# Splitting a 640-point transform by residue mod 4 in an adaLN, spectral filter and FFN block, with hand-ordered engines

## The chip, the cores and the metric

The kernel runs on one core of one Trainium2 chip. The metric is device microseconds of one execution; smaller is better.

Engines as the profile names them: PE is TensorE (matmuls), PEld its weight loads, DVE is VectorE, ACT is ScalarE, POOL is GpSimd, SP is the engine that issues DMAs. PEclk is the granted TensorE clock as a share of full speed.

## The reference, cut to what matters

The block takes scales and shifts for two layer norms from a conditioning vector `c` (this is adaLN), filters the tokens in the frequency domain, and ends in a feed-forward network (FFN).

```python
# x: [1, 2048, 640] bf16
mod = (silu(c) @ w_mod).reshape(1, 6, 1, 640)
sa, ca, ga, sb, cb, gb = mod[:, 0] ... mod[:, 5]

h = layernorm(x) * (1 + ca) + sa
X = rfft2(h)                              # over 2048 rows and 640 columns
y = irfft2(X * (w_r + 1j * w_i))          # w: [2048, 321]
x = x + ga * y

h = layernorm(x) * (1 + cb) + sb
x = x + gb * ((silu(h @ w_gate) * (h @ w_up)) @ w_down)   # 640 -> 1728 -> 640
```

The 2048 rows are held as 128 partitions times 16 values of t. The transform over the rows is done as a 128-point stage over the partitions, a 16-point stage over t, and twiddle factors folded into the 128-point tables.

## The kernel before: the parts that matter here

There are four stages.

1. Forward. For each of 16 tiles t: LayerNorm 1, five PE transposes, the transform over the 640 columns (`dfwd`), the 128-point stage (`s1`).
2. Filter. For each group of four columns: the 16-point matrix (`KS2`), the complex product with the filter on VectorE, the inverse 16-point matrix.
3. Inverse. For each tile: the 128-point stage (`vps`), the inverse column transform (`ops`), and the residual add that makes `x1`. LayerNorm 2 of the first quarter of the tiles is interleaved.
4. FFN, in four quarters of four tiles.

```python
def dfwd(t, hT):                       # forward: 10 matmuls of 324 columns
    zps = ps1.tile([P, 2, 512], F32, name="zps")
    for h in range(2):
        for c5 in range(NC5):
            nc.tensor.matmul(zps[:, h, :L], lhsT=hT[:, c5, :], rhs=Rs[:, c5, h * L:(h + 1) * L],
                             start=(c5 == 0), stop=(c5 == NC5 - 1))
    # ... Z <- zps, on VectorE or ScalarE

def stage_a(q):                        # filter, four columns
    # ... xps <- B2 times KS2
    for cp in range(2):
        in0 = xps5[:, :ni, cp].unsqueeze(2).to_broadcast([P, ni, 2, NT, 4])
        s0 = 1 - cp
        in1 = Wb[:, s0:s0 + 2, :, 16 * q:16 * q + 4 * ni].rearrange("p a k (i j) -> p i a k j", j=4)
        nc.vector.tensor_tensor(PP[:, :ni, cp], in0, in1, ALU.mult)   # L417: four neighbouring l innermost

# inverse, tile t
for h in range(2):
    ops = ps3.tile([P, 320], F32, name="ops", bufs=3)
    for ci in range(5):
        nc.tensor.matmul(ops[:], lhsT=VT[:, ci, :], rhs=Rinv_sb[:, ci, h * 320:(h + 1) * 320], ...)
    nc.vector.tensor_tensor(x1[:, t, h * 320:(h + 1) * 320], ops[:],
                            x_sb[:, t, h * 320:(h + 1) * 320], ALU.add)

# LayerNorm 2's scale and shift, on the transposed tile: columns 0, 2, 4 on VectorE, 1, 3 on ScalarE
nc.vector.tensor_scalar(h2T[:, :, c5, :], h2T[:, :, c5, :], one_p_cb[:, c5:c5 + 1], modcols[:, 2, c5:c5 + 1], ...)

# the fold of gb into w_down: 14 tensor_tensor on VectorE (L575), inside the first FFN quarter
```

## Time and profile before

| | us |
|---|---|
| before, median of the first 3 runs | 321.55 (320.47 to 322.75) |
| profiled execution, span | 319.9 |
| forward, to the first filter matmul | 65.4 |
| filter | 37.2 |
| inverse | 35.1 |
| FFN | 182.2 |

The windows view of before gives the busy time of each engine in each stage. The columns are the stretch and its length in us, then busy us of each engine with its count of instructions, the granted clock, the DMA share and GB/s.

```profile
core 0: us, PE busy (x) PEld busy (x) DVE busy (x) ACT busy (x) POOL busy (x), PEclk, DMA share, GB/s
10.50:65.40 54.90, 49.18 (x410) 33.47 (x411) 34.47 (x113) 32.09 (x59) 8.54 (x16) 0.94 0.60 219
65.40:102.50 37.10, 25.78 (x340) 21.80 (x341) 28.21 (x64) 24.02 (x46) 4.65 (x6) 0.91 0.52 127
102.50:137.70 35.20, 31.68 (x321) 24.63 (x321) 31.65 (x109) 13.35 (x20) 0.54 (x2) 1.00 0.39 137
137.70:319.90 182.20, 177.70 (x988) 96.44 (x987) 74.44 (x169) 40.28 (x66) 1.57 (x3) 1.00 0.11 27
```

TensorE is busy for 90% of the forward and inverse stages and 98% of the FFN; in the filter stage it is not, and VectorE is the busiest engine there.

### The profile page before, as it was taken

The page shows a single profiled execution, that of the slowest core. Times are in us where ns is not written, and L with a number is a line of the kernel's source. Part 1 is how long each engine was busy: PE and PEld are TensorE (multiplying, and loading weights), DVE is VectorE, ACT ScalarE, POOL GpSimd, SP SyncE. Part 2 cuts the span into 40 slices and gives each one's busy share as a digit, 9 for nine tenths or more (in the row PEclk, how much of TensorE's full clock was granted, in tenths as well). Part 3 has the DMA queues.
Part 4 walks back from the last instruction along what each step waited for, and adds up shares of the span by engine and source line. Part 5 has one row for each costly group of instructions (what it writes and reads, how often), then busy time and mean ns, then how long its engine had stood idle before and what let it go on. Part 6 is the DMA issues. An engine that isn't in the chain of part 4 may idle for free.

```text
span 319.9 us, 5193 instructions
## 1 busy us (share of the span) xinstructions
PE 285.4 (89%) x2087; PEld 177.4 (55%) x2087; DVE 172.9 (54%) x469; ACT 114.5 (36%) x197; POOL 16.3 (5%) x33
## 2 busy tenths in 40 slices
PE   0699879858666998888999999999999999999995
PEld 0477556647555786643446744457544467444574
DVE  2889563268984799899934432333233322333321
ACT  4477722745777433424222032211222200322200
POOL 1503001000202000000000000000000000000000
PEclk9999987987999999999999999999999999999999
DMA  7995900785513903113004100022100001000011
GB/s 272 416 394 203 298 29 12 287 149 119 208 72 108 423 25 61 25 36 56 0 2 102 41 31 0 1 54 71 49 2 0 0 23 41 31 0 0 0 43 41
DMA packets 26600, 29.81 MB, mean 93 GB/s; under 512 B 19521, under 2 KB 22546, under 8 KB 26450
## 3 DMA queue, kind: packets, MB, share of 16 engines
q1 hardware_dynamic: 22882, 12.66, 14.3%
q0 software_dynamic: 3040, 16.02, 13.8%
q10 hardware_dynamic: 656, 0.82, 0.9%
q8 instruction: 16, 0.26, 0.3%
q14 instruction: 6, 0.05, 0.0%
HBM read 21.86 MB, written 2.62 MB: 77 GB/s over the span
## 4 chain that ended last, share of the span: by engine, by line
PE 66%; DVE 16%; ACT 8%; DMA 7%; issue 1%; POOL 1%; SPq 0%; ACTq 0%; DVEq 0%
PE ups L567 17%; PE gps L564 16%; PE zps L314 4%; DMA Wb<-in_A_w_i_dram 4%; DVE x_1516 L536 3%; ACT Ep L436 2%; DMA x_sb<-in_A_x_dram 2%; DVE Wd_sb L575 2%; DMA h2T_all<-xn2c 2%; DVE xn2c L490 1%; PE yps L426 1%; PE yps L425 1%; PE gps L551 1%; PE xps L410 1%; PE gps__661 L362 1%
## 5 line engine op out<-in xcount | busy, mean ns | idle before, releaser
L571 DVE TENSOR_TENSOR AT<-ups,sg 128x512 bf16<-128x512 f32 x52 | 35.7, 689 | 63.2 <-PE ups L567 63.2
L567 PE MATMUL ups<-h2T_all,Wgu 128*128 128x512 bf16 x260 | 64.4, 379 | 1.3 <-DVE AT L571 1.3
L564 PE MATMUL gps<-h2T_all,Wgu 128*128 128x512 bf16 x260 | 64.4, 379 | 0.0
L570 ACT ACTIVATE sg<-gps 128x512 f32<-128x512 f32 x52 | 31.0, 597 | 73.1 <-PE gps L564 70.3
L587 PEld LDWEIGHTS <-AT 128*128 128x128 bf16 x448 | 43.8, 98 | 17.8
L567 PEld LDWEIGHTS <-Wgu 128*128 128x128 bf16 x260 | 25.4, 98 | 32.0 <-issue 1.5
L564 PEld LDWEIGHTS <-Wgu 128*128 128x128 bf16 x260 | 25.4, 98 | 30.7
L314 PE MATMUL zps<-Rs,hT 128*128 128x324 bf16 x160 | 29.4, 327 | 1.2 <-ACT hT L307 0.8
L417 DVE TENSOR_TENSOR PP<-xps,Wb 128x512 bf16<-128x512 f32 (+1 forms) x42 | 27.4, 662 | 5.4 <-ACT B_946 L405 1.8
L534 PE MATMUL ops<-Rinv_sb,VT 128*128 128x320 bf16 x160 | 24.4, 299 | 2.6 <-ACT VT L523 1.4
L314 PEld LDWEIGHTS <-hT 128*128 128x128 bf16 x160 | 16.1, 105 | 7.7 <-ACT hT L307 1.0
L534 PEld LDWEIGHTS <-VT 128*128 128x128 bf16 x160 | 15.0, 98 | 8.1 <-ACT VT L523 1.7
L523 ACT CAST VT<-vps 128x640 bf16<-128x640 f32 x16 | 10.8, 691 | 17.3 <-PE vps L521 17.3
L536 DVE TENSOR_TENSOR x_1516<-ops,x_sb 128x320 f32<-128x320 f32 x32 | 14.8, 471 | 2.2 <-PE ops L534 2.2
L307 ACT COPY hT<-t1ps 128x640 bf16<-128x640 bf16 x16 | 11.1, 697 | 6.4 <-PE t1ps L305 6.4
L329 ACT CAST A_sb<-aps 128x648 bf16<-128x648 f32 x16 | 11.2, 699 | 4.9 <-PE aps L328 4.7
L425 PE MATMUL yps<-identb,PP 128*128 128x128 bf16 x81 | 12.5, 233 | 0.0
L426 PE MATMUL yps<-identb,PP 128*128 128x128 bf16 x81 | 12.5, 233 | 0.0
L499 ACT ACTIVATE h2T_all<-h2T_all,modcols,one_p_cb 128x512 bf16<-128x512 bf16 x8 | 6.1, 806 | 14.2 <-DMA h2T_all<-xn2c 14.2
L318 DVE CAST Z<-zps 128x648 bf16<-128x648 f32 x8 | 6.5, 817 | 7.4 <-PE zps L314 5.8
L283 DVE BATCH_NORM_STATS2 st<-x_sb 128x6 f32<-128x320 bf16 x16 | 7.5, 470 | 5.5 <-DMA x_sb<-in_A_x_dram 5.5
L305 PE MATMUL t1ps<-identb,xn 128*128 128x128 bf16 x80 | 8.5, 237 | 2.2 <-POOL Ktab L229 2.2
(341 smaller groups left out, 387.1 us busy)
## 6 DMA issues: line engine op xcount, KB each, us to landing
wm<-in_w_mod_dram POOLq DMA_DIRECT2D x1, 3200.0 KB, 16.3
out_dram<-xo SPq DMA_DIRECT2D x16, 160.0 KB, 1.8
Wgu<-in_B_w_gate_dram POOLq DMA_DIRECT2D x1, 2160.0 KB, 9.1
Wgu<-in_B_w_up_dram POOLq DMA_DIRECT2D x1, 2160.0 KB, 14.9
Wd_sb<-in_B_w_down_dram POOLq DMA_DIRECT2D x1, 2080.0 KB, 9.9
x_sb<-in_A_x_dram SPq DMA_DIRECT2D x3, 640.0 KB, 8.4
Gtab<-tab_G SPq DMA_DIRECT2D x4, 384.0 KB, 8.8
Htab<-tab_H POOLq DMA_DIRECT2D x1, 1536.0 KB, 6.7
```

The source lines that it names most:

```text
L314: nc.tensor.matmul(zps[:, h, :L], lhsT=hT[:, c5, :], rhs=Rs[:, c5, h * L:(h + 1) * L], start=(c5 == 0), stop=(c5 == NC5 - 1))
L329: nc.scalar.copy(A_sb[:, :, t, :, :].rearrange("p l c j -> p c l j"), aps[:, :, :L].rearrange("p c (l j) -> p c l j", j=4),)
L417: nc.vector.tensor_tensor(PP[:, :ni, cp], in0, in1, ALU.mult)
L425: nc.tensor.matmul(yps[:, i, :], lhsT=PP[:, i, 0].rearrange("p a k j -> p (a k j)"), rhs=identb[:], start=True, stop=False)
L426: nc.tensor.matmul(yps[:, i, :], lhsT=PP[:, i, 1].rearrange("p a k j -> p (a k j)"), rhs=identb[:], start=False, stop=True)
L534: nc.tensor.matmul(ops[:], lhsT=VT[:, ci, :], rhs=Rinv_sb[:, ci, h * 320:(h + 1) * 320], start=(ci == 0), stop=(ci == 4))
L536: nc.vector.tensor_tensor(x1[:, t, h * 320:(h + 1) * 320], ops[:], x_sb[:, t, h * 320:(h + 1) * 320], ALU.add)
L564: nc.tensor.matmul(gps[:], lhsT=Wgu[:, 0, c5, fc * 128:(fc + 1) * 128], rhs=h2T[:, :, c5, :], start=(c5 == 0), stop=(c5 == NC5 - 1))
L567: nc.tensor.matmul(ups[:], lhsT=Wgu[:, 1, c5, fc * 128:(fc + 1) * 128], rhs=h2T[:, :, c5, :], start=(c5 == 0), stop=(c5 == NC5 - 1))
L570: nc.scalar.activation(sg[:], gps[:], ACT.Silu)
L571: mul_i = nc.vector.tensor_tensor(AT[:, fc, :], ups[:], sg[:], ALU.mult)
L587: nc.tensor.matmul(ops4[:], lhsT=AT[:, fc, tl * 128:(tl + 1) * 128], rhs=Wd_sb[:, fc, h * 320:(h + 1) * 320], start=(fc == 0), stop=(fc == ...
```

## The change

The intent is to take work off TensorE in the two stages that it bounds. The 640 columns are split by their residue mod 4, so that each residue has a short transform. The radix-4 butterfly that would put them together is folded into the 16-point matrices of the filter stage, where it costs no matmul. Forward, 1304 columns are streamed per tile instead of 3240; inverse, 1280 instead of 3200. A 16-point block now holds a column `l` and its partners `l+160` and, mirrored, `320-l` and `160-l`, so the products read the filter in pairs 160 elements apart and need a second, reversed copy (`Wv`), which is made by DMA through DRAM. Results of the inverse come out ordered by residue.

LayerNorm 1 is folded away too: its mean is corrected in `Z` and its `rstd` scales the table `G`, on GpSimd. Other work moves to GpSimd: LayerNorm 2's normalise of the first quarter, and the fold of `gb` into `w_down`, which before ran on VectorE during the FFN. All DMAs but one, the first load from `w_mod`, go to one queue. SBUF is laid out by hand in regions (`rX` x, `rM` products and x1, `rA` A_sb and w_down, `rE` tables and the inverse's input, `rW` filter and then FFN weights and h2T, `rL` small buffers).

```diff
 # forward
-        for h in range(2):
-            for c5 in range(NC5):
-                nc.tensor.matmul(zps[:, h, :L], lhsT=hT[:, c5, :], rhs=Rs[:, c5, h * L:(h + 1) * L],
-                                 start=(c5 == 0), stop=(c5 == NC5 - 1))
+        for h in range(2):
+            o_all = zps[0:M, h, 0:2 * RC]
+            nc.tensor.matmul(o_all, lhsT=lhs[4], rhs=R[:, 1, 2 * h:2 * h + 2, :].rearrange("p r n -> p (r n)"), ...)
+            for rr in range(2):
+                nc.tensor.matmul(zps[0:M, h, rr * RC:(rr + 1) * RC], lhsT=lhs[2 * h + rr], rhs=R[:, 0, 2 * h + rr, :], ...)
+        if t >= 2:
+            Gss[t - 2] = gscale(t - 2)                 # GpSimd, L323
+        ...                                            # Z, and the variance, on VectorE
+        nc.gpsimd.tensor_tensor(rstd[:, t:t + 1], vt, mhalf[:], ALU.pow)   # L341
 ... (cut)
 # filter products
-        in1 = Wb[:, s0:s0 + 2, :, 16 * q:16 * q + 4 * ni].rearrange("p a k (i j) -> p i a k j", j=4)
-        nc.vector.tensor_tensor(PP[:, :ni, cp], in0, in1, ALU.mult)
+        for hl in range(2):
+            in0 = xv[:, :n, hl, cp].unsqueeze(2).to_broadcast([P, n, 2, NT, 2])
+            if hl == 0:
+                in1 = _rev(Wn, base + ls[0], [[st, n], [NT * NW, 2], [NW, NT], [160, 2]])
+            else:
+                in1 = _rev(Wv, base + 255 - ls[0], [[-st, n], [NT * NW, 2], [NW, NT], [-160, 2]])
+            nc.vector.tensor_tensor(PP[:, :n, cp, hl], in0, in1, ALU.mult)   # L470
 ... (cut)
 # inverse
-            nc.vector.tensor_tensor(x1[:, t, h * 320:(h + 1) * 320], ops[:], x_sb[:, t, h * 320:(h + 1) * 320], ALU.add)
+            dv = "p (m h r) -> p h r m"
+            nc.vector.tensor_tensor(x1[:, t, :].rearrange(dv, h=2, r=2),
+                                    ops[:, :, 0:320].rearrange("p h (r m) -> p h r m", r=2),
+                                    x_sb[:, t, :].rearrange(dv, h=2, r=2), ALU.add)     # L649
 ... (cut)
+            if t == 9:
+                ln2_norm_pool()
+                for tl in range(4):
+                    ln2_xn(tl, nc.gpsimd)
+                ln2_tr(0)
+            if t == NT - 1:
+                ln2_mod(0)                             # L616, L619: scale and shift h2T
+        for f2 in range(NFC):                          # before: on VectorE, in the first FFN quarter
+            m = 128 if f2 < 13 else 64
+            nc.gpsimd.tensor_tensor(Wd_sb[:m, f2, :], Wd_sb[:m, f2, :], gb_bc[:m, :], ALU.mult)   # L663
```

## The prediction

> **What bounds it now.** The timeline of TensorE splits the 319.9 us into four stages.
> - Forward transform, to about 65 us. Per tile t: five transposes, ten 324-column matmuls (1.38 us start to start), four more (0.55): 2.2 us, TensorE back to back. Set-up takes 12 us; about 10 us is lost from 30 to 53 us, around the 11.9 us filter load in the chain of waits, the modulation matmuls and a clock of 0.76 to 0.81 (windows).
> - Filter, 66 to 102.5 us. VectorE paces it: 0.67+0.67+0.17 us per four columns, 1.51 us period, 21 times.
> - Inverse, 102.5 to 137.7 us. TensorE: ten 128-column matmuls 0.056 us apart and ten 320-column ones 0.136 us apart, 1.91 us per tile; plus stalls around LN2.
> - FFN, 137.7 us to the end: 44.36 us per quarter, matmuls back to back (last three quarters 133.1 us); the first quarter loses 1.6 us to the Wd fold on VectorE.
>
> The Trainium skill ("TensorE: Matmul & The Clock Gate", back-to-back issue gap) gives N/2.4+2.5 ns; the trace agrees (0.136 us at 320 columns, 0.056 at 128).
>
> **What changes.** The residue split makes the d transforms sparse: 1304 streamed columns per tile instead of 3240 forward, 1280 instead of 3200 inverse. That saves about 0.82 us of TensorE per tile each way, 13 us + 13 us. The radix-4 butterfly rides in the existing 16-point matrices: the filter stage keeps its 81 blocks, matmul count and products (0.67 us each). LN1's normalise pass, bn_stats and sqrt go; a sum of squares, five tiny operations and a scaling of G on GpSimd come.
>
> **By stage.**
> - Forward: TensorE falls to about 1.35 us per tile. ScalarE (hT 0.70 + A_sb 0.70 + half a Square 0.75) and VectorE (Z 0.82, half a square-sum 0.75, five tiny at 0.15) are both near 1.8. I take 1.9 to 2.0 with latencies, start near 11 us, plus 2 us for sa: ends near 47 us (saves 18).
> - Filter: VectorE needs 27 us of products, but the depth is one group: xps(g+1) queues behind two yps/copy/eps rounds, about 2.9 us per eight columns. The ga, gb, cb modulation matmuls move in (6 us). 36 to 38 us, nothing saved. Extra DMA: the filter is copied reversed through DRAM and read twice in 512-byte rows. From the old 642-byte load (4096 rows in about 11 us) I estimate 8 to 10 us for each of flip, normal and reversed read. All queue on SP ahead of wm_r (3.3 MB), tables and the transposes. wm_r lands near 54, transposes near 60: a stall of about 5 us. Ends near 91.
> - Inverse: 1.15 us per tile, but the LN2 sums on ScalarE make the first four 2.2 to 2.3. 24 us. LN2 of chunk 0 starts at tile 9 (GpSimd normalise 4 us, transpose 4.9 us): about 3 us stall. FFN starts near 118.
> - FFN: 4 x 44.36 + 3.2 = 180.7 us. Wd fold on GpSimd: the skill ("GPSIMD Engine Reference", elementwise accounting) has two-input operations at about 2.6 cycles per element; estimate 1.4 us x 14, hidden behind the 29 us before the first down projection.
>
> Sum: about 298 us.
>
> **Right or wrong in the profile.** Forward period under 2.1 us, TensorE gaps released by ScalarE and VectorE; filter stage near 37 us, DMA releasing gps/B2 reads; ops line near half its busy time; FFN quarters of 44.4 us.
>
> **What would make it wrong.** Slower: 512-byte DRAM-to-DRAM flips, a 4096-element GpSimd negation, TensorE dropping to its low clock in the thinner stages. Faster: DMA early enough, filter loop at VectorE's 2.66 us.
>
> Predicted 298 us, 8 in 10 between 285 and 310; faster by over 2%: 0.92, within 2%: 0.06, slower: 0.02.

## More of the kernel before

The groups view names the costly work: line, engine, operation, output and input, count; then busy us and mean ns of one; then idle time of the engine just before it and what ended that.

```profile
L314 PE MATMUL zps<-Rs,hT 128*128 128x324 bf16 x160 | 29.4, 327 | 1.2 <-ACT hT L307 0.8
L417 DVE TENSOR_TENSOR PP<-xps,Wb 128x512 bf16<-128x512 f32 (+1 forms) x42 | 27.4, 662 | 5.4 <-ACT B_946 L405 1.8
L534 PE MATMUL ops<-Rinv_sb,VT 128*128 128x320 bf16 x160 | 24.4, 299 | 2.6 <-ACT VT L523 1.4
L536 DVE TENSOR_TENSOR x_1516<-ops,x_sb 128x320 f32<-128x320 f32 x32 | 14.8, 471 | 2.2 <-PE ops L534 2.2
L496 DVE TENSOR_SCALAR h2T_all<-h2T_all,one_p_cb,modcols 128x512 bf16<-128x512 bf16 x12 | 4.3, 405 | 4.4 <-DMA h2T_all<-xn2c 4.4
```

L314 and L534 are the column transforms that the change makes sparse. Keep three other numbers in mind for later: a filter product (L417), a residual add (L536, 471 ns for 320 elements) and LayerNorm 2's scaling (L496, 405 ns for 512). The mean of L417 mixes two shapes; the view by form has the products of 512 elements alone at 681 ns:

```profile
L417 DVE TENSOR_TENSOR PP<-xps,Wb 128x512 bf16<-128x512 f32 x40 | 26.9, 681 | 5.3 <-ACT B_946 L405 1.8 <-PE xps L410 1.6 <-PE yps L426 0.6
```

## The result, and the profile after

| | median us | runs |
|---|---|---|
| before | 321.01 | 4, 318.42 to 322.75 |
| after | 337.36 | 4, 335.92 to 337.81 |

The ratio is 1.0535 with a 95% interval of 1.0463 to 1.0607: 5% slower. (A ratio here is the mean time of one kernel's fast runs over that of the other's of the same rounds, so it is not quite the ratio of the medians quoted.) The prediction of 298 us was wrong in sign, and 39 us too low.

The windows view of after, with stretches cut at the same events (the first cut lies 0.2 us before the first filter matmul, at 54.3); the fourth stretch is new:

```profile
10.50:54.10 43.60, 29.16 (x277) 21.22 (x276) 28.11 (x97) 24.79 (x43) 24.00 (x34) 0.99 1.00 324
54.10:104.30 50.20, 34.21 (x413) 27.33 (x413) 41.58 (x56) 34.59 (x49) 19.19 (x23) 0.84 0.50 106
104.30:135.50 31.20, 20.76 (x256) 17.99 (x256) 20.36 (x21) 16.96 (x32) 9.39 (x9) 0.94 0.42 133
135.50:149.90 14.40, 0.01 (x1) 0.04 (x2) 14.40 (x2) 1.52 (x2) 14.34 (x12) 0.50 0.00 0
149.90:334.10 184.20, 180.58 (x988) 97.28 (x988) 82.88 (x195) 39.93 (x66) 1.84 (x4) 0.98 0.11 27
```

The TensorE saving came: 49.2 busy us fell to 29.2 in the forward stage and 31.7 to 20.8 in the inverse. The stages did not follow. Forward fell by 11.1 us and the inverse by 3.9; the filter stage grew by 12.8 (37.2 to 50.0), 14.4 us of almost nothing came before the FFN, and the FFN grew by 2.0. Together that is 14.2 us, the difference of the two spans (334.1 against 319.9).

The groups of after that answer to those of before:

```profile
L470 DVE TENSOR_TENSOR rM<-xps,rW 128x512 bf16<-128x512 f32 (+2 forms) x44 | 38.4, 950 | 3.3 <-PE xps L458 3.3
L649 DVE TENSOR_TENSOR rM<-ops,rX 128x640 f32<-128x640 f32 x16 | 19.6, 1332 | 8.0 <-PE ops L646 8.0
L616 DVE TENSOR_SCALAR rW<-rW,one_p_cb,modcols 128x512 bf16<-128x512 bf16 x12 | 18.5, 1598 | 1.5 <-DMA rW<-rL 1.5
L663 POOL TENSOR_TENSOR rA<-rA,gb_bc 128x640 bf16<-128x640 bf16 (+1 forms) x14 | 18.9, 1393 | 0.0
L674 PE MATMUL gps<-rW,Wp_1292 128*128 128x512 bf16 x20 | 6.0, 440 | 17.4 <-DVE rW L616 17.4
L351 PE MATMUL aps<-rE 128*128 128x324 bf16 x16 | 5.0, 313 | 12.2 <-POOL rE L323 12.2
```

The mean of L470 again mixes shapes. By form, its products of 512 elements alone:

```profile
L470 DVE TENSOR_TENSOR rM<-xps,rW 128x512 bf16<-128x512 f32 x36 | 33.9, 1021 | 3.3 <-PE xps L458 3.3
```

Four things stand out. A filter product of 512 elements takes 1021 ns where it took 681. A residual add takes 1332 ns for 640 elements where two of 320 took 942. The mean scaling of h2T is 1598 ns where it was 405. And TensorE waits 17.4 us for that scaling, and 12.2 us for GpSimd's scaling of `G`.

The mean of L616 hides its shape. Of twelve instructions the shortest took 404 ns, the median 409 and the longest 14128. The timeline of after around that one (start, length, engine, line, idle time before with what ended it):

```profile
133.25 16.23 POOL L663 TENSOR_TENSOR rA<-rA,gb_bc 128x640 bf16<-128x640 bf16 x12
135.50 1.52 ACT L619 ACTIVATE rW<-rW,modcols,one_p_cb 128x512 bf16<-128x512 bf16 x2 [4.03 <-DMA rW<-rL]
135.50 15.35 DVE L616 TENSOR_SCALAR rW<-rW,one_p_cb,modcols 128x512 bf16<-128x512 bf16 x3 [1.47 <-DMA rW<-rL]
149.89 2.29 PE L674 MATMUL gps<-rW,Wp_1292 128*128 128x512 bf16 x5 [17.40 <-DVE rW L616]
```

ScalarE does two of the five scalings in 1.52 us. VectorE starts its first at the same moment and is done with it only when GpSimd's last fold is (133.25 + 16.23 = 149.48). The chain of waits of after in that stretch (start, length, what) has the same story:

```profile
127.99 2.58 POOL rL L605 x3
130.58 0.03 POOL rA L663
130.60 4.88 DMA rW<-rL
135.48 0.03 issue
135.50 14.14 DVE rW L616
149.64 0.25 issue
149.89 2.29 PE gps L674 x5
```

### The profile page after: what moved, and what is told of

It is laid out like the page before. It is cut to its first block, busy times and chain, and to the rows that moved or that the text cites. A ratio compares the mean times of both kernels' runs of the same rounds, so it can differ in the third digit from the quotient of the medians.

```text
span 334.1 us, 4983 instructions
## 1 busy us (share of the span) xinstructions
PE 267.1 (80%) x1973; PEld 166.0 (50%) x1973; DVE 190.9 (57%) x385; ACT 122.2 (37%) x200; POOL 71.2 (21%) x86
## 4 chain that ended last, share of the span: by engine, by line
PE 54%; DVE 7%; DMA 2%; ACT 2%; POOL 1%; issue 1%; POOLq 0%; DVEq 0%
PE ups L690 16%; PE gps L687 16%; DVE rW L616 4%; DVE rM L649 2%; PE gps L674 2%; DMA rW<-rL 1%; DMA rE<-rE 1%; POOL rL L605 1%; ACT rL L584 1%; ACT rL L633 1%; ACT rL L585 1%; PE ops_3089 L713 1%; PE ops_3073 L713 1%; PE ops_3040 L713 1%; PE ops_3023 L713 1%
## 5 line engine op out<-in xcount | busy, mean ns | idle before, releaser
L690 PE MATMUL ups<-rW 128*128 128x512 bf16 x260 | 65.4, 383 | 0.4 <-DVE rX L694 0.4
L687 PE MATMUL gps<-rW 128*128 128x512 bf16 x260 | 65.7, 384 | 0.0
L693 ACT ACTIVATE rE<-gps 128x512 f32<-128x512 f32 x52 | 31.0, 597 | 76.8 <-PE gps L687 70.1
L690 PEld LDWEIGHTS <-rW 128*128 128x128 bf16 x260 | 25.7, 99 | 32.0 <-issue 2.1
L687 PEld LDWEIGHTS <-rW 128*128 128x128 bf16 x260 | 25.7, 99 | 31.6 <-issue 1.6
L470 DVE TENSOR_TENSOR rM<-xps,rW 128x512 bf16<-128x512 f32 (+2 forms) x44 | 38.4, 950 | 3.3 <-PE xps L458 3.3
L713 PEld LDWEIGHTS <-rE 128*128 128x128 bf16 x224 | 21.9, 98 | 8.8
L713 PEld LDWEIGHTS <-rX 128*128 128x128 bf16 x224 | 21.9, 98 | 8.8
L649 DVE TENSOR_TENSOR rM<-ops,rX 128x640 f32<-128x640 f32 x16 | 19.6, 1332 | 8.0 <-PE ops L646 8.0
L674 PE MATMUL gps<-rW,Wp_1292 128*128 128x512 bf16 x20 | 6.0, 440 | 17.4 <-DVE rW L616 17.4
L616 DVE TENSOR_SCALAR rW<-rW,one_p_cb,modcols 128x512 bf16<-128x512 bf16 x12 | 18.5, 1598 | 1.5 <-DMA rW<-rL 1.5
L663 POOL TENSOR_TENSOR rA<-rA,gb_bc 128x640 bf16<-128x640 bf16 (+1 forms) x14 | 18.9, 1393 | 0.0
L341 POOL TENSOR_TENSOR rstd<-vtmp,mhalf 128x1 f32<-128x1 f32 x16 | 12.8, 798 | 27.0 <-DVE vtmp L340 26.0
L478 PE MATMUL yps<-identb,rM 128*128 128x128 bf16 x162 | 13.7, 242 | 3.3 <-DVE rM L470 3.3
L355 ACT CAST rA<-aps 128x648 bf16<-128x648 f32 x16 | 11.1, 702 | 12.7 <-PE aps L354 12.7
L351 PE MATMUL aps<-rE 128*128 128x324 bf16 x16 | 5.0, 313 | 12.2 <-POOL rE L323 12.2
## 6 DMA issues: line engine op xcount, KB each, us to landing
rM<-in_w_mod_dram SPq DMA_DIRECT2D x1, 3200.0 KB, 13.1
```

What stands on the lines that cost most here:

```text
L341: nc.gpsimd.tensor_tensor(rstd[:, t:t + 1], vt, mhalf[:], ALU.pow)
L470: nc.vector.tensor_tensor(PP[:, :n, cp, hl], in0, in1, ALU.mult)
L478: nc.tensor.matmul(yps[:, i, :], lhsT=PP[:, o4 + i, cp].rearrange("p h a k m -> p (h a k m)"), rhs=identb[:], start=(cp == 0), stop=(cp == 1))
L649: nc.vector.tensor_tensor(x1[:, t, :].rearrange(dv, h=2, r=2), ops[:, :, 0:320].rearrange("p h (r m) -> p h r m", r=2), x_sb[:, t, :].rear ...
L663: nc.gpsimd.tensor_tensor(Wd_sb[:m, f2, :], Wd_sb[:m, f2, :], gb_bc[:m, :], ALU.mult)
L687: nc.tensor.matmul(gps[:], lhsT=Wgu[:, 0, c5, fc * 128:(fc + 1) * 128], rhs=h2T[:, :, c5, :], start=(c5 == 0), stop=(c5 == NC5 - 1))
```

## The experiments

The theory after reading the traces has four parts: (1) GpSimd's fold holds a port that VectorE's fast scaling needs ("port theory" in the expectations; what it rests on is named under e2); (2) reading the filter 160 elements apart makes each product slow ("line theory"; see under e3); (3) writing `x1` in residue order makes each add slow; (4) the order of GpSimd's own program delays `G`. The rivals: GpSimd's long chain slows everyone, or h2T is late for another reason; the products or adds are slow because of how PSUM is read; the forward stage is bound by ScalarE and VectorE, as predicted.

Every edit is a diff against the kernel after, or against the experiment named. The starts of the stages in all runs, in us, read from the first matmul of each in the timeline:

| run | filter | inverse | FFN | length of filter stage |
|---|---|---|---|---|
| before | 65.4 | 102.6 | 137.7 | 37.2 |
| after | 54.3 | 104.3 | 149.9 | 50.0 |
| e1_fold_vector | 55.1 | 104.2 | 136.0 | 49.1 |
| e2_mod_scalar | 54.4 | 104.3 | 136.2 | 49.9 |
| e3_w_pair | 54.4 | 96.2 | 141.6 | 41.8 |
| e4_x1_order | 55.8 | 105.7 | 151.5 | 49.9 |
| e5_x1_write | 57.5 | 107.3 | 151.6 | 49.8 |
| e6_gs_early | 45.5 | 98.8 | 144.5 | 53.3 |
| e7_sa_early | 54.9 | 101.8 | 147.5 | 46.9 |
| e8_comb | 45.6 | 94.6 | 122.0 | 49.0 |
| e9_reorder | 54.5 | 96.4 | 140.6 | 41.9 |
| e10_all | 46.0 | 90.0 | 116.7 | 44.0 |
| e11_deep | 46.1 | 90.7 | 117.4 | 44.6 |
| e12_order | 45.7 | 87.8 | 113.4 | 42.1 |

The forward stage of one kernel varies by up to 3 us between executions (e5 changes nothing in it), so a few us of a later start mean nothing unless the stage itself is named.

### The fold back on VectorE: e1_fold_vector

```diff
-        for f2 in range(NFC):
-            m = 128 if f2 < 13 else 64
-            nc.gpsimd.tensor_tensor(Wd_sb[:m, f2, :], Wd_sb[:m, f2, :], gb_bc[:m, :], ALU.mult)
 ... (in the FFN, after the product of block fc)
+                if sc == 0:
+                    for f2 in ([fc] if fc < 12 else [12, 13]):
+                        m = 128 if f2 < 13 else 64
+                        nc.vector.tensor_tensor(Wd_sb[:m, f2, :], Wd_sb[:m, f2, :], gb_bc[:m, :], ALU.mult)
```

> Edit: the 14 folds of gb into Wd leave GpSimd and go to VectorE, one after each of the first FFN quarter's products. Port theory[...]: the first h2T scaling on VectorE falls from 14.1 us to about 0.4, the FFN starts about 13 us earlier (near 137 instead of 149.9), and the total falls from about 337 to about 324. Rival (the scaling waits for the transposed tile or for x1, not for GpSimd): the FFN still starts near 150 and the total stays within 2 us of 337.

Timed: 323.28 us median (before beside it: 318.58), ratio 1.0143, 1.0077 to 1.0209: still slower than before, by an amount that the 2% verdict calls unclear. The timeline of this run where after had the hole:

```profile
135.31 1.06 DVE L616 TENSOR_SCALAR rW<-rW,one_p_cb,modcols 128x512 bf16<-128x512 bf16 x3 [1.49 <-DMA rW<-rL]
135.98 2.29 PE L671 MATMUL gps<-rW,Wp 128*128 128x512 bf16 x5 [3.68 <-DVE rW L616]
```

Three scalings now take 1.06 us, and the FFN starts 13.9 us earlier, though h2T arrives at the same time (135.3 against 135.5). So the hole belongs to the fold on GpSimd, and not to a late h2T. The five matmuls still take 2.29 us, twice their later 1.24.

### The scaling moved instead, the fold kept: e2_mod_scalar

```diff
         for c5 in range(NC5):
-            if c5 % 2 == 0:
+            if c5 % 2 == 0 and sc > 0:
```

> Edit: GpSimd keeps the folds; only the three VectorE scalings of the first h2T chunk move to ScalarE. Port theory: [...]five scalings take about 4.1 us from 135.5 and the FFN starts near 140, about 10 us earlier; total near 327. Rival (while GpSimd folds, everyone's SBUF access is slow): the five ScalarE scalings take well over 0.8 us each and most of the 14 us stays.

This keeps GpSimd as it is and takes VectorE out of the chain: ScalarE does all five scalings of the first quarter. It took 329.72 us (one run). The timeline:

```profile
133.14 9.51 POOL L663 TENSOR_TENSOR rA<-rA,gb_bc 128x640 bf16<-128x640 bf16 x7
135.38 3.63 ACT L619 ACTIVATE rW<-rW,modcols,one_p_cb 128x512 bf16<-128x512 bf16 x5 [4.03 <-DMA rW<-rL]
136.24 3.40 PE L674 MATMUL gps<-rW,Wp 128*128 128x512 bf16 x5 [3.88 <-ACT rW L619]
```

ScalarE works at its usual pace while the folds run, and so does TensorE (from 142.73 its groups of five matmuls take 1.24 us); the folds themselves still take 1388 to 1419 ns. The rival "everyone is slow beside GpSimd" falls. VectorE as a whole is not slowed either: in after three residual adds, which read PSUM and one SBUF tensor, ran beside the first folds in 1327 to 1353 ns, against a median of 1330 for all. With e1 this pins the hole to the pair of GpSimd's fold and VectorE's scaling.

But the FFN started 13.7 us earlier than in after and the profiled span fell by only 6.2 (334.1 to 327.9). The folds caught another VectorE instruction, a product of two SBUF tensors in the first FFN quarter (views of VectorE and of TensorE):

```profile
142.97 6.96 DVE L682 TENSOR_TENSOR rE<-rE 64x512 bf16<-64x512 bf16 x1 [9.07 <-DMA rE<-rE]
150.58 2.29 PE L690 MATMUL ups<-rW 128*128 128x512 bf16 x5 [4.45 <-DVE rE L694]
```

It takes 0.68 us in e1, and here it ended after the last fold. TensorE waited 4.45 us behind it and began again at half its pace, so the FFN took 191.7 us where e1's takes 184.8. So the folds block more than the scaling, and moving only the scaling away moves the wait.

The Trainium skill names a mechanism that fits ("SBUF — State Buffer", Who interferes with whom): VectorE's two-port modes and GpSimd share a pair of SBUF ports under an exclusive lock, and `tensor_scalar` can be in such a mode. The page says that whoever issues first has the pair "for the whole instruction". The trace agrees that the other blocks fully, but shows more: VectorE waited not for one fold of 1.4 us but for the rest of one and some ten more, back to back (from 135.50 to 149.48). No run counts port grants, so the lock itself is the page's; what the runs show is who slows whom.

### The filter pair made neighbours: e3_w_pair

```diff
-  in1 = _rev(Wn, base + ls[0], [[st, n], [NT * NW, 2], [NW, NT], [160, 2]])
+  in1 = _rev(Wn, base + ls[0], [[st, n], [NT * NW, 2], [NW, NT], [1, 2]])
 ... (the same for Wv, -160 to -1)
```

> Edit, wrong result on purpose: in the filter products the two filter values of a pair are read 1 element apart instead of 160 apart; PSUM input, output and all run lengths stay. Line theory[...]: the product falls from 0.94 to about 0.66 us and the filter stage from 50 to about 39 us. Rival 1 (runs of two elements cost an extra cycle per run, on whatever operand): stays at 0.94. Rival 2 (GpSimd's rotations running beside it slow it): stays at 0.94.

The values are wrong: the wrong filter column is read. (The output still passed the comparison with the reference, whose tolerance therefore does not see the filter stage's values in this problem.)

```profile
L470 DVE TENSOR_TENSOR rM<-xps,rW 128x512 bf16<-128x512 f32 (+2 forms) x44 | 26.4, 666 | 6.2 <-PE xps L458 6.2
L470 DVE TENSOR_TENSOR rM<-xps,rW 128x512 bf16<-128x512 f32 x36 | 23.3, 711 | 6.2 <-PE xps L458 6.2
```

One stride alone, 320 bytes to 2, takes the product of 512 elements (second line, by form) from 1021 to 711 ns; the PSUM read and the write are unchanged. The products give back 12.0 us of VectorE and the stage 8.2 of it (50.0 to 41.8): waits for `xps` grew from 3.3 to 6.2 us. The Trainium skill has 16-byte lines in SBUF and says that accesses that hit a different line each time pay ("Advanced Engine Details and Errata", SBUF Cachelines). The run agrees, and puts a size to it: about 0.31 us in 512 elements.

### How the residual add reads and writes: e4_x1_order and e5_x1_write

```diff
 # e4: the same add, elements visited in output order; PSUM is read in hops of 640 bytes
-            dv = "p (m h r) -> p h r m"
-            nc.vector.tensor_tensor(x1[:, t, :].rearrange(dv, h=2, r=2),
-                                    ops[:, :, 0:320].rearrange("p h (r m) -> p h r m", r=2),
-                                    x_sb[:, t, :].rearrange(dv, h=2, r=2), ALU.add)
+            nc.vector.tensor_tensor(x1[:, t, :].rearrange("p (m h r) -> p m h r", h=2, r=2),
+                                    ops[:, :, 0:320].rearrange("p h (r m) -> p m h r", r=2),
+                                    x_sb[:, t, :].rearrange("p (m h r) -> p m h r", h=2, r=2), ALU.add)
 # e5: only the write made contiguous (the values land in the wrong places)
-            nc.vector.tensor_tensor(x1[:, t, :].rearrange(dv, h=2, r=2),
+            nc.vector.tensor_tensor(x1[:, t, :].rearrange("p (h r m) -> p h r m", h=2, r=2),
```

> Edit, right result: the add that makes x1 runs over the same elements in the order of its output, so write and x read are contiguous and the PSUM read hops 640 bytes between neighbours. If only the SBUF write step cost, 1.31 us falls to about 0.8. If PSUM reads off their line cost too, it stays at 1.2 or more. The result also tells whether the filter products could run over PSUM in another order.

> Edit, wrong result on purpose: the add that makes x1 writes its 640 f32 results contiguously instead of 16 bytes apart; PSUM read and the x read (8 bytes apart) stay. Write theory: 1.31 us falls to about 0.79. Rival (the 8-byte step of the bf16 x read costs): stays near 1.3. If both cost, in between. Total at most 6 us lower, less because the first four tiles are held by ScalarE.

The group of the add in e4, then in e5:

```profile
L648 DVE TENSOR_TENSOR rM<-ops,rX 128x640 f32<-128x640 f32 x16 | 13.1, 824 | 13.1 <-PE ops L646 13.0
```

```profile
L649 DVE TENSOR_TENSOR rM<-ops,rX 128x640 f32<-128x640 f32 x16 | 13.1, 823 | 11.7 <-PE ops L646 11.6
```

Both take 0.82 us instead of 1.33. In e5 only the write differs from after, `x_sb` is still read 8 bytes apart and PSUM in order; so the write, f32 values 16 bytes apart, is the whole cost. In e4 PSUM is read in hops, and that costs nothing. e4 is correct; e5 is not (relative error 1.41).

The totals did not move: 337.53 and 337.59 us. The adds were not what the time hung on. ScalarE's LayerNorm 2 sums hold the first four tiles at 2.2 us, VectorE's idle time before the adds grew from 8.0 to 13.1 and 11.7 us, and the end of the inverse was followed by the wait for the fold chain, whose end sets the FFN's start.

### GpSimd's order in the forward stage: e6_gs_early

In after, GpSimd's program has the scaling of `G` for tile t−2 behind the power of tile t−1, which waits for VectorE. The timeline of after in one such tile, GpSimd first, then TensorE:

```profile
31.34 1.06 POOL L341 TENSOR_TENSOR rstd<-vtmp,mhalf 128x1 f32<-128x1 f32 x1 [1.33 <-DVE vtmp L340]
32.40 0.58 POOL L323 TENSOR_SCALAR rE<-rE,rstd 128x384 bf16<-128x384 bf16 x1
33.03 0.32 PE L351 MATMUL aps<-rE 128*128 128x324 bf16 x1 [1.38 <-POOL rE L323]
```

```diff
-            if t >= 2:
-                Gss[t - 2] = gscale(t - 2)
             ...
             nc.gpsimd.tensor_tensor(rstd[:, t:t + 1], vt, mhalf[:], ALU.pow)
+            Gss[t] = gscale(t)
```

> Edit: on GpSimd the scaling of G for tile t follows tile t's power at once, instead of queueing behind the powers of tiles t+1 and t+2's turn. Queue theory (TensorE's 12.2 us of waits for the scaled G in the forward stage come from this order): these waits fall under 3 us and the forward stage ends 2 to 4 us before 54.1; VectorE, near 1.96 us per tile, is then the limit. Rival (VectorE is the limit already and the waits only show it): the waits move elsewhere and the stage ends within 1 us of 54.

The wait view of TensorE over the forward stage:

```profile
PE aps L350 <- POOL rE L323: 3.3, 6, 1.5
```

The wait fell from 12.2 to 3.3 us, and the stage ended at 45.5 instead of 54.3: 8.8 us, where I had expected 2 to 4 (e8 to e12, which carry this edit, end it at 45.6 to 46.1). Of these, 3.3 were given back in the filter stage (53.3 instead of 50.0), where TensorE now waits 2.3 us in its modulation matmuls for the load of `w_mod`. The total was 329.26 us (one run).

### The `sa` add moved ahead of the products: e7_sa_early

```diff
-            if g >= 3:
-                B2b, i, l0, nb = B2of[ls[0]]
-                if l0 not in seen:
-                    seen.add(l0)
-                    nc.vector.tensor_tensor(B2b[:, :nb, 0:1], B2b[:, :nb, 0:1], SA[:, l0:l0 + nb].unsqueeze(2), ALU.add)
 ... (after the matmuls into xps, before the products)
+            if g in (2, 4, 6, 8):
+                B2b, i, l0, nb = B2of[groups[g + 1][0]]
+                nc.vector.tensor_tensor(B2b[:, :nb, 0:1], B2b[:, :nb, 0:1], SA[:, l0:l0 + nb].unsqueeze(2), ALU.add)
```

> Edit: the small add of SA to the next transposed batch goes before the previous group's products on VectorE instead of behind them. If it is the cause of the five gaps of 0.7 to 1.1 us (xps waiting for rL L454), they vanish and the filter stage falls from 50.2 to about 46.5 us; VectorE then runs its 44 products back to back, at 0.94 us each. If the gaps stay, their cause is another.

The transform of the shift `sa` (SA) is added to each new batch of transposed columns. In after, that small add stands in VectorE's queue behind the products of the group before, and TensorE needs its result for the next `xps`: a bubble of 0.7 to 1.1 us for each batch of 16 columns. With the add earlier VectorE never waits:

```profile
L468 DVE TENSOR_TENSOR rM<-xps,rW 128x512 bf16<-128x512 f32 (+2 forms) x44 | 38.6, 947 | 0.0
```

The stage fell by 3.1 us, to 46.9, with the products as slow as before; the total was 332.64 us (one run).

### The waits together: e8_comb

This is e1, e6 and e7 together, with LayerNorm 2's two sums on ScalarE spread over the first eight inverse tiles, one per tile, instead of two in each of the first four.

```diff
-            if t < 4:
-                ln2_stats_act(t)
-            if t == 9:
+            if t < 8:
+                ln2_stats_act(t // 2, t % 2)
+            if t == 8:
```

> All of: folds on VectorE, scaled G early, SA add early, the LN2 sums of chunk 0 one per tile over eight tiles instead of two per tile over four. From 323.3 by about 3 + 3.5 + 1.5: near 315 to 316, about 1 to 1.5 per cent under the kernel before. If the gaps hide behind one another, 318 to 320.

Timed: 308.26 us median, ratio 0.9701, 0.963 to 0.9772. The FFN starts at 122.0, which is 27.9 us before after's: 8.7 from the forward stage, 1.0 from the filter stage, 18.2 from the inverse and the hole behind it. This is the first version that beats before, and it is better than I had expected.

### The slow accesses removed, with correct values: e9_reorder

Eight neighbouring columns become the innermost dimension of the products, instead of the pair 160 apart, and the add goes in e4's order.

```diff
-            PP = rM.cut(4096 * (g % 3), [8, 2, 2, 2, NT, 2])
+            PP = rM.cut(4096 * (g % 3), [2, 2, 2, NT, 2, 8])
-                    in0 = xv[:, :n, hl, cp].unsqueeze(2).to_broadcast([P, n, 2, NT, 2])
+                    in0 = xv[:, :n, hl, cp].rearrange("p i k m -> p k m i").unsqueeze(1).to_broadcast([P, 2, NT, 2, n])
-                        in1 = _rev(Wn, base + ls[0], [[st, n], [NT * NW, 2], [NW, NT], [160, 2]])
+                        in1 = _rev(Wn, base + ls[0], [[NT * NW, 2], [NW, NT], [160, 2], [st, n]])
 ... (the same for Wv; yps reads PP[:, cp, :, :, :, :, o4 + i])
```

> Edit of the changed kernel alone, right result: both layout costs undone. x1 add in output order (as e4), and the filter products run with eight neighbouring frequencies innermost, so W is read and PP written contiguously and only the PSUM read hops (512 bytes). Line theory plus free PSUM hops: products 0.66 us instead of 0.94, filter stage 50 to about 41 to 45; total about 327 to 329, as e3. Rival (PSUM hops cost in this shape, or TensorE pays for reading PP as weights 16 bytes apart): products stay above 0.8, or yps waits appear and the stage stays above 46.

```profile
L470 DVE TENSOR_TENSOR rM<-xps,rW 128x512 bf16<-128x512 f32 (+2 forms) x44 | 25.8, 648 | 6.9 <-PE xps L458 6.8
L470 DVE TENSOR_TENSOR rM<-xps,rW 128x512 bf16<-128x512 f32 x36 | 22.4, 684 | 6.9 <-PE xps L458 6.8
```

The product of 512 elements takes 684 ns although it now reads PSUM in hops of 512 bytes; the filter stage is 41.9 us, as in e3. For the filter's values this run and e10 to e12 rest on reading the loops: each product keeps its pair of operands. TensorE pays a little: the weight loads of `yps` from the products, now 16 bytes apart, take 148 ns instead of 110. The total was 325.73 us (one run), with after's hole still in it.

### Both together, and two attempts at what is left: e10_all, e11_deep, e12_order

e10_all is e8_comb with e9_reorder's two edits, no other.

> e8 with both reorderings. If the layout costs add to the other three: 308 minus 5 to 10 for the products and 3 to 4 for x1: 296 to 300. If TensorE or the one-group-deep filter loop binds once VectorE is faster: 301 to 304.

Timed: 301.53 us median, ratio 0.9408, 0.9347 to 0.947. In its filter stage the DMA stall that I had predicted for after is plain (TensorE had waited 2.3 us for it in e6 and 1.9 in e8): TensorE waits 2.9 us for `w_mod`, and VectorE 2.4 us for the transposed columns that queue behind it.

e11_deep adds to e10 one more group of depth between the inverse 16-point matrix and its copy, and issues the modulation matmuls two steps later:

```diff
-            if it < 5:
-                mods2(it)
+            if 2 <= it < 7:
+                mods2(it - 2)
 ... (stage_c and rot of group g one iteration later)
```

> e10 with eps one group later (a deeper loop, four Y2 buffers) and the modulation matmuls two iterations later, behind the landing of wm_r. Loop theory: the xps waits of the filter stage fall under 1 us and the 2 to 3 us wait for wm_r goes: 4 to 6 us below e10. If e10 has no such waits, equal within 1 us.

It gained nothing: 302.72 us, ratio 0.9471, 0.9413 to 0.9528, with a filter stage of 44.6 us against 44.0. A hole of 4.35 us for the transposes stayed, because the order of the DMAs had not changed.

e12_order leaves the depth of e10 and changes that order: the loads of `w_mod`'s rest, `RI` and `H` go behind the first three transposes, and the modulation matmuls to steps 6 to 10.

```diff
-    nc.sync.dma_start(wm_r[:], wm_v[:, :, 2 * D:6 * D].rearrange("p k (i d) -> p k i d", i=4))
-    nc.sync.dma_start(RI[:], RI_dram)
-    nc.sync.dma_start(Htab[:], H_dram)
 ... (after the first three t2_dma)
+        nc.sync.dma_start(wm_r[:], wm_v[:, :, 2 * D:6 * D].rearrange("p k (i d) -> p k i d", i=4))
+        nc.sync.dma_start(RI[:], RI_dram)
+        nc.sync.dma_start(Htab[:], H_dram)
-            if it < 5:
-                mods2(it)
+            if 6 <= it < 11:
+                mods2(it - 6)
```

> e10 with the load of wm_r and the two inverse tables issued behind the first three transposes instead of before them, and the ga, gb, cb modulation matmuls moved from the first five filter steps to steps 6 to 10. Theory (in e10 the two holes of 3.6 and 2.5 us at the start of the filter stage are DMA: wm_r first, then transposes that queued behind it): both holes go, filter stage 44 to about 39 us, total 296 to 298 against e10's 301.5. Rival (the holes come from TensorE's order or the transposes' own time): within 1 us of e10. It may also be that wm_r now lands too late and step 6 waits.

Timed: 299.47 us median (before beside it: 319.9), ratio 0.9383, 0.9322 to 0.9445. It is the fastest version, 6.2% faster than before. The step from e10 is 2 us, and the intervals of the two ratios overlap; that the holes went is read from the stage. The windows of e12_order, cut at the same events:

```profile
9.00:45.70 36.70, 28.87 (x277) 21.28 (x277) 29.47 (x106) 26.12 (x47) 24.70 (x34) 1.00 0.91 274
45.70:87.80 42.10, 32.98 (x412) 27.88 (x412) 29.51 (x56) 33.80 (x48) 19.09 (x23) 0.84 0.94 253
87.80:113.40 25.60, 19.94 (x256) 16.57 (x257) 14.61 (x24) 16.68 (x33) 5.48 (x8) 1.00 0.43 135
113.40:297.10 183.70, 179.54 (x988) 96.86 (x988) 87.65 (x209) 40.93 (x68) 1.04 (x2) 0.99 0.11 27
```

Forward, inverse and hole are as they should be. The filter stage is 42.1 us, not the 39 that I had expected, and still 4.9 longer than before's. In it ScalarE is now the busiest engine, at 33.8 us against before's 24.0, with TensorE close behind at 33.0. Its copies of the inverse's input (L492; PSUM read in hops of 512 bytes, written in runs of four bf16) take up to 1.44 us; before, copies of 512 elements took 0.59 with the same runs but PSUM in order. In after they take 0.73 and 1.28 to 1.45 us by turns, and by the layout the runs of every second copy lie across a 16-byte boundary. The reading order of PSUM is not the reason: in the same run the copies of L494 have the same hops, with runs that by the layout start on 8-byte boundaries, and take 0.59 us. Two copies of L492 and one of L494, by form:

```profile
L492 ACT CAST rE<-eps__930 128x512 bf16<-128x512 f32 x1 | 1.4, 1437 | 0.0
L492 ACT CAST rE<-eps__924 128x512 bf16<-128x512 f32 x1 | 0.8, 789 | 0.0
L494 ACT CAST rE<-eps__781 128x512 bf16<-128x512 f32 x1 | 0.6, 591 | 0.0
```

That the place of the runs is the reason, and that ScalarE binds the stage now, is argued from these numbers and not tested by a run.

## Why the prediction was wrong

The predicted time was 298 us and the measured one 336 to 338. The profiled span was 334.1, and the difference of 36 us has these parts.

| step, as the prediction put it | predicted | measured in after | shown by |
|---|---|---|---|
| forward "ends near 47" | 47 | 54.3 | e6: 45.5 with GpSimd's order changed |
| filter "36 to 38 us, nothing saved", stall of 5, "ends near 91" | 91 | 104.3 | e3: 41.8, e9: 41.9, with the products at 0.71 and 0.68 us |
| inverse 24, stall of 3, "FFN starts near 118" | 27 | 31.2, to the arrival of h2T | e8: 27.4 with the fold gone and LayerNorm 2 earlier |
| Wd fold "hidden behind the 29 us before the first down projection" | 0 | 14.4 | e1, e2 |
| FFN 180.7 | 180.7 | 184.2 | windows, timeline |

The parts: 7 us forward, 6 more in the filter stage, 4 in the inverse, 14 in the hole, 3.5 in the FFN. That is 35, and the rest is rounding. In the filter stage two errors partly cancel: the predicted 44 us contain a stall of 5 that did not come in after, so the slow products cost more than the 6 us that show.

**Wrong: the fold was costed but not what it does to others.** This is the largest term. The cost was right: the Trainium skill ("GPSIMD Engine Reference", 3.1 Elementwise) has two-input operations at about 2.6 cycles an element, from which I estimated 1.4 us, and the trace has 1.393 us. That TensorE would not need the result for 29 us was also right. But a chain of 19 us on GpSimd is not hidden when it blocks an instruction of VectorE on TensorE's path. e1 removes 13.9 us of hole by moving the fold, e2 removes 13.7 by moving the scaling (and loses 7.5 again in the FFN, where the folds block the next instruction). The page on SBUF that says so was in my reach when I predicted.

**Wrong: products kept at "0.67 us each".** The number of products was nearly kept (42, then 44) and the elements exactly, but the innermost stride went from 2 bytes to 320. The product of 512 elements measured 1.02 us against 0.68 before; e3 gives back 0.31 us of it by changing that stride alone. The prediction checked the arithmetic and not the access patterns. The residual add is the same error, 1.33 us for 640 elements against 0.82 (e4, e5), but in after it was nearly free because other things held the stage.

**Wrong: forward "1.9 to 2.0 us".** The balance of ScalarE and VectorE was about right. What failed was the unstated assumption that GpSimd's small work would be ready in time. In GpSimd's program order the scaling of `G` stood behind a power that waits for a later tile; TensorE lost 12.2 us to it. e6 takes the stage to 45.5 us, better than the 47 predicted. The sign given for it, "TensorE gaps released by ScalarE and VectorE", was wrong too: GpSimd released them.

**Wrong in after, right behind it: the DMA stall of 5 us.** In after the filter stage started late enough to hide it. Once it started at 45.5 to 46.0, TensorE waited for `w_mod` 2.3 us in e6 and 2.9 in e10, where VectorE waited 2.4 more for the transposes.

**Off in size: the inverse.** The slow adds are not its 4 us: from its start to the arrival of h2T e4, with fast adds, takes 31.4 us (105.7 to 137.1). e8, which spreads LayerNorm 2's sums and normalises a tile earlier, takes 26.7 (94.6 to 121.3) with the adds still slow. So the schedule of LayerNorm 2 is the likelier cause; no run changed it alone.

**Off in size: the FFN.** Of its 3.5 us, about 3 are the start at half clock: PEclk was 0.50 in the hole, and the first five matmuls took 2.29 us where before took 1.24. The first three groups of five started 2.08, 2.14 and 1.88 us apart, later ones 1.08, which makes 2.9 us. It does not take the whole hole: in e1 TensorE had waited 3.7 us, started as slowly, and the FFN took 184.8 us. The Trainium skill ("TensorE: Matmul & The Clock Gate", Part 1: The HAM clock gate) says that an idle TensorE falls to half its clock, and the trace agrees.

**Right.** The saving on TensorE: its busy time fell from 285.4 to 267.1 us, and where nothing else binds, late in e12's inverse, a tile takes 1.11 us (from 105.54 to 106.65), near the predicted 1.15, where it took 1.91. (Earlier tiles of e12 take 1.31: there ScalarE's copy and LayerNorm 2 sum follow each other without a gap.) (The matmul group of the inverse transform did not fall to "near half its busy time", though: 24.4 us became 9.6 + 9.5, because the records overlap: one of 320 columns lasts 0.30 us and the next matmul starts 0.135 us later, so each run of matmuls adds its last tail; a count of starts is the better sign.) ScalarE holding the first four inverse tiles at 2.2 us. And, with luck, the size of the prize: e12 has 299.5 us, close to the 298 predicted. But e12 is after with seven more edits, and its errors against the prediction cancel: its stages end at 45.7, 87.8 and 113.4 where the prediction had 47, 91 and 118, and its FFN takes 183.7 instead of 180.7. Nor was before tuned in the same way. So the runs show that after's schedule and layouts cost it some 38 us (337.4 to 299.5), and not how much of the lead over before belongs to the split alone.

## What to carry to other kernels

When work moves to an engine that "has time", ask which instructions of other engines run beside it, not only whether its result is needed; one long chain of GpSimd beside a fast VectorE instruction cost more here than the whole chain would have cost on VectorE (14.4 us against 5.7). When a change keeps the count of elements, compare the innermost stride of every operand with the one before; here it was worth 0.31 us in 512 elements, and the order of loops alone won it back. When a mean is odd, look at minimum, median and maximum of the group: eleven at 0.4 and one at 14 us is a wait, not a cost.

## What the Trainium skill lacked or had wrong

- "SBUF — State Buffer", Who interferes with whom, says that the port pair is held for the whole instruction. It does not say who has it next when one side has more instructions ready. Here VectorE's `tensor_scalar`, usually 0.41 us, took 14.13 us, until some ten more GpSimd two-input instructions of 1.39 us, back to back, had all ended. In e2 a `tensor_tensor` with two SBUF inputs took 6.96 us instead of 0.68 in the same way.
- "VectorE: DVE Perf Modes", Mode 1×, says that "fp32, weird strides, PSUM operands — all work", and names no cost of the strides. Measured: a bf16 SBUF operand read 320 bytes apart took 512 elements from 0.71 to 1.02 us; an f32 result written 16 bytes apart took 640 elements from 0.82 to 1.33 us. The rule is on another page ("Advanced Engine Details and Errata", SBUF Cachelines), without a size; sizes for 4-byte elements do stand in "Vector Engine (DVE) Microarchitecture Reference", 5.2 Measured stream behaviour on trn2.
- "Advanced Engine Details and Errata", PSUM Cachelines, speaks of non-contiguous access as slow for matmuls and says nothing of VectorE. VectorE reading PSUM in hops of 640 and 512 bytes cost nothing: 824 ns in e4 (823 in e5 without the hops) and, for 512 elements, 684 in e9 (711 in e3).
- I found no page with the time of a GpSimd power on one element per partition. It took 0.55 us, and 1.06 in the six cases in which VectorE's square sum with two SBUF inputs ran beside it (the latter agrees with the rule in "SBUF — State Buffer").
- I found no page with the cost of weight loads from a strided tile (110 ns became 148 at 16 bytes apart), or of ScalarE's access patterns: copies of 512 elements that read PSUM in hops of 512 bytes and write runs of four bf16 took 0.59 us with the runs on 8-byte boundaries, 0.73 off them, and up to 1.45 us where by the layout the runs lie across a 16-byte boundary.
